# Exchanged halves of the partitions for the odd pairs of heads from the second batch on instead of from the third

## The chip, the cores and the metric

The kernel runs on one core of a Trainium2 chip. The metric is device time in microseconds (us) from the start to the end of one execution. Beside it stands the span of a profiled execution, which is the time from its first to its last instruction.

## The reference: what is computed

Four batches of eight heads go through a retention layer (attention scores with a decay and no softmax), then through two feed-forward blocks. Only the retention is touched by the change. Cut to what matters:

```python
scores = scale * np.matmul(q, k.transpose(0, 1, 3, 2))       # q, k, v: 4 x 8 x 576 x 64
gamma = 1.0 - 2.0 ** (-5.0 - np.arange(H, dtype=np.float32))
rel = pos[:, None] - pos[None, :]
Dmat = np.where(rel >= 0, gamma[:, None, None] ** rel[None, :, :], 0.0)
attn = np.matmul(scores * Dmat, v)
x = attn.transpose(0, 2, 1, 3).reshape(B * S, H * D)         # 2304 x 512
h = (x @ w1) * (x @ w2) @ w3 @ w_out
g = h @ w_in                                                 # then a leaky unit and a last product
```

## The kernel before

**How the work is tiled.** Two heads form a pair, one on partitions 0 to 63 and one on 64 to 127, so a batch has four pairs. The 576 positions of a batch are cut into five chunks, four of 128 and one of 64. The class `Retention` has three kinds of work for a chunk `c`. `scores` (L287, L276) multiplies keys by queries; VectorE then multiplies the result by the decay `mask` and gives `rt` (L291; for the last chunk `mtail` and `rte`, L279). `moments` (L302) and the state `S` (L310, L312, with the factor `gc`) carry what earlier chunks add. `values` adds two products in PSUM: state times queries (L333, 64 x 64 blocks of the array) and values times `rt` (L342). VectorE reads the PSUM tile `o` into `xs` (L349), and ScalarE and VectorE split `xs` into `xh` and `xl` for the next product.

**Where a head stands.** `places` says for each head of a pair from which partitions its operands come and to which it writes. Uncrossed, a head on partitions 0 to 63 writes to 0 to 63, and so does each pair; L333 then uses two of the four 64 x 64 blocks of the array. Crossed, the odd pairs have their heads on the other half, so that an odd and an even pair use all four. A crossed batch needs the keys, queries and last values of the odd pairs loaded in halves of 64 partitions (`in_places`, L382), and the odd pairs' columns of `mask`, `mtail` and `gc` exchanged once. That is `cross`, twelve small DMAs. Before the change batches 0 and 1 are uncrossed, and 2 and 3 crossed.

**The order of the work.** Batch 0 runs alone. Then `ab_unit` (L179) multiplies `x` by the columns of `w12`; each of its two products per column is followed by a step of the next batch's retention (`cycle`). Batch 1 has seven steps in six such places, so that its last two, for chunks 3 and 4, follow each other directly. PE, ACT and SP run in the order written; VectorE's order is made when the kernel is built. A weight of `w12` is prepared by ACT (L93, L94, L112) and VectorE (L103 to L108, L116); L112 writes its upper and L116 its lower part.

**The loads.** All go out on SP's queue. For batch 1, pairs 2 and 3 are loaded early into the room of weights (`load_apart`, tiles `pair`), pairs 0 and 1 when batch 0 has freed theirs (`load_pair`, tiles `qk` and `kv`). ACT scales the keys of a batch by `kd` (`prep`, L265). `raw` are weights as they come from HBM.

**PSUM.** Uncrossed, a chunk's `o` is one bank, and there are two of them. Crossed, it is two banks, and there is one such tile.

Of the kernel before, what the change touches and what calls it, by code (L numbers as in the profile page):

```python
# [13 lines left out]
PSUM = bass.MemoryType.PSUM  # L14
# [3 lines left out]
B, H, S, D = 4, 8, 576, 64  # L18
NPAIR = H // 2
NT, DM, DF1, DF2 = B * S, 512, 1024, 2048  # L20
CH = 128
# [116 lines left out]
def retention_moe_kernel(ctx: ExitStack, tc, qk, kv, w_out1, w3t, w12, w_in, w_out2, alpha, c_row, c_pair, out):  # L138
    nc = tc.nc

    def pool(stack, name, bufs=1, **kw):
        return stack.enter_context(tc.tile_pool(name=name, bufs=bufs, **kw))
# [20 lines left out]
    def flush():  # L163

        todo = later[:]
        later.clear()
        for step in todo:
            step()
# [17 lines left out]
    def in_wa(i, name):  # L186
        return wa.tile([P, 2, DM], F32R, tag=f"wa{i}", name=name)
# [39 lines left out]
    mtail = per_pair[:, :, 2 * CH:2 * CH + 64]  # L227
    qs = per_pair[:, :, 2 * CH + 64:]
    per_row = decay.tile([P, 128], F32, name="per_row")[:, 0:H + NPAIR]
    kd, gc = per_row[:, 0:H], per_row[:, H:]  # L230
# [11 lines left out]


    def crossed(b):
        return b >= 2

    def places(b, p):

        x = p % 2 if crossed(b) else 0
        return [(HEADS[(j + x) % 2], HEADS[j], (j + x) % 2) for j in range(2)]  # L250

    class Retention:
# [64 lines left out]
        def values(self, c):  # L317
            b, n = self.b, self.n
            w = CH if c < NCH - 1 else 64
            i0 = c * CH  # L320
            q, v, rt = qt[b], kvt[b], self.rt.pop(c)
            two = crossed(b)
            if two:
                o = self.psum["o"].tile([P, 2, 2, 2 * CH], F32, tag="o", name=f"o{b}_{c}")
                o = o[:, :, 0].rearrange("p r (i w) -> p r i w", w=CH)
            else:
                o = self.psum["o"].tile([P, NPAIR, CH], F32, tag="o", name=f"o{b}_{c}", bufs=2)
                o = o.rearrange("p (i r) w -> p r i w", r=2)
            clears = range(2 if two else 1)
            if c:  # L330
                for m, p in enumerate(self.pairs):
                    for rows, pp, _ in places(b, p):
                        nc.tensor.matmul(o[pp, p % 2, m // 2, 0:w], self.state[c - 1][rows, m],  # L333
                                         q[p][rows, i0:i0 + w],
                                         start=(m in clears), stop=False, skip_group_check=True)
            for m, p in enumerate(self.pairs):
                for j, (rows, pp, r) in enumerate(places(b, p)):
                    if c < NCH - 1:
                        vj, rj = v[p][:, 8 + 4 * j + c], rt[:, r, m]
                    else:  # L340
                        vj, rj = vt[b][p][rows], rt[rows, m]
                    nc.tensor.matmul(o[pp, p % 2, m // 2, 0:w], vj, rj, start=(c == 0 and m in clears), stop=True,  # L342
                                     skip_group_check=True)
            later.append(lambda: self.decayed(c, o, w))
# [32 lines left out]
    qt, kt, kvt, vt = ({b: {} for b in range(B)} for _ in range(4))  # L377

    def in_places(b, p, t, src):

        for rows, pp, _ in places(b, p):
            nc.sync.dma_start(out=t[rows], in_=src[pp])  # L382

    def cross():

        for p in range(1, NPAIR, 2):
            in_places(2, p, gc[:, p:p + 1], c_row[:, H + p:H + p + 1])
            for h in range(2):
                nc.sync.dma_start(out=mask[:, h, p], in_=c_pair[:, p, (1 - h) * CH:(2 - h) * CH])
            in_places(2, p, mtail[:, p], c_pair[:, p, 2 * CH:2 * CH + 64])  # L390

    def load_pair(b, p):
        x = attn.tile([P, 2, S], F32, tag=f"qk{p}", name=f"qk{b}_{p}")
        y = attn.tile([P, 17, D], F32, tag=f"kv{p}", name=f"kv{b}_{p}")
        qt[b][p], kt[b][p], kvt[b][p], vt[b][p] = x[:, 0], x[:, 1], y[:, 0:16], y[:, 16]
        if crossed(b) and p % 2:
            in_places(b, p, x, qk[b, p])
            nc.sync.dma_start(out=y[:, 0:16], in_=kv[b, p, :, 0:16])
            in_places(b, p, y[:, 16], kv[b, p, :, 16])
        else:  # L400
            nc.sync.dma_start(out=x, in_=qk[b, p])
            nc.sync.dma_start(out=y, in_=kv[b, p])
        if b == 0:
            nc.sync.dma_start(out=per_pair[:, p], in_=c_pair[:, p])

    def load_apart(b, p, n):

        x, y, z = (in_wa(n + m, f"pair{b}_{p}_{m}").bitcast(F32).rearrange("p a b -> p (a b)") for m in range(3))
        qt[b][p], kt[b][p] = x[:, 0:S], y[:, 0:S]
        vt[b][p] = x[:, S:S + D]  # L410
        kvt[b][p] = z.rearrange("p (a d) -> p a d", d=D)
        nc.sync.dma_start(out=qt[b][p], in_=qk[b, p, :, 0])
        nc.sync.dma_start(out=kt[b][p], in_=qk[b, p, :, 1])
        nc.sync.dma_start(out=kvt[b][p], in_=kv[b, p, :, 0:16])
        nc.sync.dma_start(out=vt[b][p], in_=kv[b, p, :, 16])

    def load_batch(b):
        for p in range(NPAIR):
            load_pair(b, p)

    def attention_psum(stack, twice):
        return {"sc": pool(stack, f"ps_sc{twice}", bufs=twice, space=PSUM, reuse_waits="tile"),
                "st": pool(stack, f"ps_st{twice}", space=PSUM, reuse_waits="tile"),
                "o": pool(stack, f"ps_o{twice}", space=PSUM, reuse_waits="tile") if twice == 2 else None}
# [10 lines left out]
    load_pair(0, 3)  # L435
    nc.sync.dma_start(out=al, in_=alpha)
    load_apart(1, 2, 10)
    load_apart(1, 3, 13)
    warm = psum0["o"].tile([P, 512], F32, tag="o", name="warm", bufs=2)
    for _ in range(16):  # L440
# [18 lines left out]
        flush()  # L459
    flush()  # L460
    flush()
    first.close()


    pm = pool(ctx, "pm", bufs=3, space=PSUM, reuse_waits="tile")
    pap = ExitStack()
    psum1 = attention_psum(pap, 1)
# [49 lines left out]
    def retention(b):  # L517
        r = Retention(b, list(range(NPAIR)), psum1)
        return Steps([r.prep] + r.steps())

    first_o = ExitStack()
    psum1["o"] = pool(first_o, "ps_o1", space=PSUM, reuse_waits="tile")
    r = retention(1)
    between = cycle(r, 7 / 6, 1, 6)
    for c in range(3):
# [2 lines left out]
    r.rest()  # L528
    flush()
    flush()  # L530
    first_o.close()
    psum1["o"] = pool(pap, "ps_o3", space=PSUM, reuse_waits="tile")
    cross()
    load_batch(2)
    between = cycle(None, 0, 0.6)
    for c in range(3):
# [592 lines left out]
```

## Time and profile before

| | before |
|---|---|
| three runs | 803.22, 806.06, 806.58 us; median 806.06 |
| the profiled execution | 803.67 us, span 801.9 us |
| PE busy | 787.3 us (98%) |
| PE weight loads busy | 694.1 us (87%) |
| VectorE busy | 497.7 us (62%) |
| ACT busy | 348.6 us (43%) |
| mean granted clock of PE | 0.996 |

The profiled execution lies 1.8 us outside its span and 2.4 us under the median of the runs. PE's share is an average; what a stage is worth has to be read from the waits of that stage.

### The profile page before, as it was taken

To read this page: it belongs to the slowest core of one execution; us is meant where nothing else is said; L and a number is where in the kernel's file an instruction comes from. 1 tells how busy PE (TensorE), PEld (TensorE's weight loads), DVE (VectorE), ACT (ScalarE), POOL (GpSimd) and SP (SyncE) were. 2 spreads that over 40 slices of the span, in tenths; PEclk is the share of its full clock that TensorE was granted. 3 is DMA by queue.
4 is the path that set the end of the run, shared out by engine and by line. 5 is a ranking of instruction groups with operands and counts; after the bars stand their busy time and mean duration, and the time that the engine had idled before them with its cause. 6 is when DMAs were issued, how large, how long until landed. Compare 5 with 4: busy or idle time off the path is not lost.

```text
span 801.9 us, 12688 instructions
## 1 busy us (share of the span) xinstructions
PE 787.3 (98%) x4768; PEld 694.1 (87%) x4768; DVE 497.7 (62%) x895; ACT 348.6 (43%) x648; POOL 0.2 (0%) x4
## 2 busy tenths in 40 slices
PE   7999999999999999999999999999999999999998
PEld 4778888888888988999999999999987888888886
DVE  4796785325477788988843677587899933222232
ACT  3553562231255565656514465465666622222121
POOL 0000000000000000000000000000000000000000
PEclk8999999999999999999999999999999999999999
DMA  9844931571366659899916925225557635344341
GB/s 345 344 158 125 356 135 54 165 249 54 123 193 183 198 197 336 296 388 407 387 63 221 352 101 196 108 96 202 182 196 239 218 99 177 106 132 138 99 136 41
DMA packets 81341, 156.24 MB, mean 195 GB/s; under 512 B 9600, under 2 KB 57728, under 8 KB 81280
## 3 DMA queue, kind: packets, MB, share of 16 engines
q1 hardware_dynamic: 81280, 155.43, 55.7%
q8 instruction: 37, 0.61, 0.3%
q14 instruction: 24, 0.20, 0.1%
HBM read 104.02 MB, written 51.38 MB: 194 GB/s over the span
## 4 chain that ended last, share of the span: by engine, by line
PE 89%; DVE 5%; DMA 2%; ACT 1%; issue 1%; SPq 1%; ACTq 0%; DVEq 0%
PE ps L179 25%; PE o L1044 23%; PE h L883 18%; PE y L816 12%; PE pw L630 5%; PE o L342 2%; PE sc L287 2%; DMA raw<-in_w_dram 1%; PE o L333 1%; PE st L302 1%; DMA gr<-gd 0%; DVE gl L173 0%; DVE xs L349 0%; DMA xs<-x2d 0%; DVE rt L291 0%
## 5 line engine op out<-in xcount | busy, mean ns | idle before, releaser
L179 PE MATMUL ps<-xh,w 128*128 128x512 f32 (+1 forms) x640 | 186.0, 372 | 2.0 <-ACT w L112 1.6
L1044 PE MATMUL o<-wb,gh 128*128 128x512 f32 x576 | 177.6, 389 | 0.9 <-ACT gh L172 0.9
L179 PEld LDWEIGHTS ps<-xh,w 128*128 128x128 f32 x640 | 116.0, 189 | 23.6 <-ACT w L112 1.8
L1044 PEld LDWEIGHTS o<-wb,gh 128*128 128x128 f32 x576 | 108.1, 188 | 23.8 <-ACT gh L172 1.4
L179 PE MATMUL ps<-xl,w 128*128 128x512 f32 (+1 forms) x320 | 118.0, 369 | 0.0
L1044 PE MATMUL o<-wb,gl 128*128 128x512 f32 x288 | 112.3, 390 | 0.4 <-DVE gl L173 0.4
L173 DVE TENSOR_TENSOR gl<-gr,gh 128x768 fp32r<-128x768 f32 x48 | 46.0, 958 | 99.9 <-ACT gh L172 99.8
L816 PE MATMUL y<-yab,wp 128*128 128x384 f32 x576 | 100.0, 334 | 0.0
L816 PEld LDWEIGHTS y<-yab,wp 128*128 128x128 f32 x576 | 99.9, 188 | 0.1
L172 ACT CAST gh<-gr 128x768 fp32r<-128x768 f32 x48 | 40.2, 838 | 115.9 <-PE o L1044 112.6
L179 PEld LDWEIGHTS ps<-xl,w 128*128 128x128 f32 x320 | 60.4, 189 | 9.8 <-DVE xl L173 0.3
L1044 PEld LDWEIGHTS o<-wb,gl 128*128 128x128 f32 x288 | 54.1, 188 | 12.3 <-DVE gl L173 1.3
L895 DVE SCALAR_TENSOR_TENSOR g<-m,al,g 128x384 f32<-128x384 f32 x48 | 29.7, 618 | 48.9 <-ACT g L894 45.8
L883 PE MATMUL h<-xT,wv 128*128 128x384 f32 x288 | 54.9, 334 | 1.5 <-DVE g L901 1.5
L883 PE MATMUL h<-xT,wu 128*128 128x384 f32 x288 | 55.0, 335 | 0.5 <-ACT h L908 0.3
L883 PEld LDWEIGHTS h<-xT,wv 128*128 128x128 f32 x288 | 50.3, 188 | 1.8 <-DVE g L901 1.8
L108 DVE CUSTOM_DVE_ANT_0 a<-a,b 128x1024 uint16<-128x1024 uint16 x72 | 49.5, 688 | 3.5
L883 PEld LDWEIGHTS h<-xT,wu 128*128 128x128 f32 x288 | 50.2, 188 | 1.1 <-ACT h L908 0.6
L487 ACT CAST ab<-f 128x512 fp32r<-128x512 f32 (+1 forms) x40 | 23.1, 577 | 63.1 <-DVE f L491 54.5
L103 DVE TENSOR_SCALAR a<-a 128x512 f32<-128x512 f32 x72 | 30.4, 422 | 25.7 <-ACT a L93 25.4
L491 DVE TENSOR_TENSOR f<-f,ps 128x512 f32<-128x512 f32 (+1 forms) x40 | 25.3, 632 | 31.6 <-PE ps L179 31.3
L630 PE MATMUL pw<-wo,w 128*128 128x512 f32 x192 | 44.1, 390 | 0.0
(95 smaller groups left out, 1007.5 us busy)
## 6 DMA issues: line engine op xcount, KB each, us to landing
gd<-g SPq DMA_DIRECT2D x96, 192.0 KB, 1.9
gr<-gd SPq DMA_DIRECT2D x96, 192.0 KB, 2.6
abd<-ab SPq DMA_DIRECT2D x32, 512.0 KB, 4.3
raw<-in_w_out_dram SPq DMA_DIRECT2D x24, 512.0 KB, 3.7
yab<-abd SPq DMA_DIRECT2D x24, 384.0 KB, 7.9
raw<-in_w_dram SPq DMA_DIRECT2D x16, 512.0 KB, 7.1
raw<-in_w3t_dram SPq DMA_DIRECT2D x16, 512.0 KB, 4.1
rawi<-in_w_in_dram SPq DMA_DIRECT2D x16, 512.0 KB, 6.3
```

The costliest lines, as they stand in the source:

```text
L103: nc.vector.tensor_scalar(out=a, in0=a, scalar1=self.LEAST, scalar2=self.MOST, op0=ALU.max, op1=ALU.min)
L108: nc.vector.tensor_tensor(out=a.bitcast(I32), in0=a.bitcast(I32), in1=b, op=ALU.add)
L172: nc.scalar.copy(hi, src)
L173: nc.vector.tensor_tensor(out=lo, in0=src, in1=_f32(hi), op=ALU.subtract)
L179: nc.tensor.matmul(ps, a, bb, start=(n == 0), stop=(n == last))
L487: nc.scalar.copy(t[:, 0], f)
L491: nc.vector.tensor_tensor(out=f, in0=f, in1=pss[1], op=ALU.mult)
L630: nc.tensor.matmul(acc[i], a[:, ic], bb, start=(k == 0 and n == 0), stop=(k == C1 - 1 and n == 2))
L816: nc.tensor.matmul(ys[o], wpc[c][a][:, oc], yab[b, c][:, bb], start=(c == 0 and i == 0), stop=(c == C1 - 1 and i == 2))
L883: nc.tensor.matmul(ps, a[:, x, ks], b[:, y, k], start=(fresh and n == 0), stop=(n == 5), skip_group_check=True)
L895: nc.vector.scalar_tensor_tensor(out=g, in0=r, scalar=neg[:, c:c + 1], in1=g, op0=ALU.mult, op1=ALU.add)
L1044: nc.tensor.matmul(accs[b][i], x[:, m, ic], y, start=(j == 0 and m == 0 and q == 0), stop=(j == C1 - 1 and m == 1 and q == 2))
```

## The change

`crossed` is true from batch 1 on. `cross` is called when batch 0 is done, ahead of the first `ab_unit`, and no longer after batch 1. `load_apart` loads queries, keys and last values in halves, those of the even pair 2 too. The one PSUM pool for `o` with two banks serves batches 1 to 3.

```diff
     def crossed(b):
-        return b >= 2
+        return b >= 1
...
     def cross():

         for p in range(1, NPAIR, 2):
-            in_places(2, p, gc[:, p:p + 1], c_row[:, H + p:H + p + 1])
+            in_places(1, p, gc[:, p:p + 1], c_row[:, H + p:H + p + 1])
             for h in range(2):
                 nc.sync.dma_start(out=mask[:, h, p], in_=c_pair[:, p, (1 - h) * CH:(2 - h) * CH])
-            in_places(2, p, mtail[:, p], c_pair[:, p, 2 * CH:2 * CH + 64])
+            in_places(1, p, mtail[:, p], c_pair[:, p, 2 * CH:2 * CH + 64])
...
-        nc.sync.dma_start(out=qt[b][p], in_=qk[b, p, :, 0])
-        nc.sync.dma_start(out=kt[b][p], in_=qk[b, p, :, 1])
+        in_places(b, p, qt[b][p], qk[b, p, :, 0])
+        in_places(b, p, kt[b][p], qk[b, p, :, 1])
         nc.sync.dma_start(out=kvt[b][p], in_=kv[b, p, :, 0:16])
-        nc.sync.dma_start(out=vt[b][p], in_=kv[b, p, :, 16])
+        in_places(b, p, vt[b][p], kv[b, p, :, 16])
...
     flush()
     flush()
+    cross()
     first.close()
...
-    first_o = ExitStack()
-    psum1["o"] = pool(first_o, "ps_o1", space=PSUM, reuse_waits="tile")
+    psum1["o"] = pool(pap, "ps_o3", space=PSUM, reuse_waits="tile")
     r = retention(1)
...
-    first_o.close()
-    psum1["o"] = pool(pap, "ps_o3", space=PSUM, reuse_waits="tile")
-    cross()
     load_batch(2)
```

PE and ACT keep their order. On SP's queue, the loads of batch 1's pair 2 stood so before (`pair_2_0` holds queries and last values, `pair_2_1` keys, `pair_2_2` the rest; what a row waits for stands in brackets, and `DMAHW0` to `DMAHW7` count the landings of every eighth DMA):

```order
L412 DMA pair_2_0_134<-in_qk_dram 128x576 [waits DMAHW0_49]
L413 DMA pair_2_1_135<-in_qk_dram 128x576 [waits DMAHW1_49]
L414 DMA pair_2_2_136<-in_kv_dram 128x1024 [waits DMAHW2_49]
L415 DMA pair_2_0_134<-in_kv_dram 128x64 [waits DMAHW3_49]
L412 DMA pair_3_0_141<-in_qk_dram 128x576 [waits DMAHW4_49]
```

The same place of SP's queue now, for pair 2:

```order
L382 DMA pair_2_0_134<-in_qk_dram 64x576 [waits DMAHW0_49]
L382 DMA pair_2_0_134<-in_qk_dram 64x576 [waits DMAHW1_49]
L382 DMA pair_2_1_135<-in_qk_dram 64x576 [waits DMAHW2_49]
L382 DMA pair_2_1_135<-in_qk_dram 64x576 [waits DMAHW3_49]
L414 DMA pair_2_2_136<-in_kv_dram 128x1024 [waits DMAHW4_49]
L382 DMA pair_2_0_134<-in_kv_dram 64x64 [waits DMAHW5_49]
L382 DMA pair_2_0_134<-in_kv_dram 64x64 [waits DMAHW6_49]
```

Three loads of 128 partitions became six of 64; each waits for the DMA eight places ahead of it. Pair 3 is changed in the same way, and pair 1's load of `qk` is cut in two and that of `kv` in three.

SP's queue behind the load of batch 1's pair 1, now (the load of the large part of `kv_1` stands eight DMAs ahead of the second `64x64` row below, and its landing is what `DMAHW6` counts there; `per_row` is the tile of `gc`, and `per_pair` that of `mask` and `mtail`):

```order
L382 DMA per_row<-const_row_dram 64x1 [waits DMAHW1_49,DVE_49]
L382 DMA per_row<-const_row_dram 64x1 [waits DMAHW2_49]
L389 DMA per_pair<-const_pair_dram 128x128 [waits DMAHW3_49,DVE_49]
L389 DMA per_pair<-const_pair_dram 128x128 [waits DMAHW4_49]
L382 DMA per_pair<-const_pair_dram 64x64 [waits DMAHW5_49,DVE_49]
L382 DMA per_pair<-const_pair_dram 64x64 [waits DMAHW6_49]
L382 DMA per_row<-const_row_dram 64x1 [waits DMAHW7_49,DVE_49]
L382 DMA per_row<-const_row_dram 64x1 [waits DMAHW0_49]
L389 DMA per_pair<-const_pair_dram 128x128 [waits DMAHW1_49,DVE_49]
L389 DMA per_pair<-const_pair_dram 128x128 [waits DMAHW2_49]
```

These rows stood ahead of batch 2's loads before; they now stand between batch 1's loads and the seventh piece of `raw`. The waits on `DVE` are for batch 0's last reads of the tables.

VectorE's queue where batch 1's first scores are masked (`rt_0`), before:

```order
L491 TENSOR_TENSOR f_0_488<-f_0_488,ps_0_1_522 128x512 [waits PE_49,Activation_49]
L291 TENSOR_TENSOR rt_0_538<-sc_0_537,per_pair 128x1024 [waits PE_49]
L103 TENSOR_SCALAR a_518<-a_518 128x512 [waits Activation_49]
L308 COPY S_0_611<-st_0_547 128x256 [waits PE_49]
L483 TENSOR_TENSOR ab_0_489<-f_0_488,ab_0_489 128x512 [waits Activation_49]
L116 TENSOR_TENSOR w_2_558<-a_484,w_2_558 128x512 [waits Activation_49]
```

The same rows of VectorE's queue now:

```order
L492 TENSOR_TENSOR f_0_509<-f_0_509,ps_0_1_543 128x512 [waits PE_49,Activation_49]
L291 TENSOR_TENSOR rt_0_559<-sc_0_558,per_pair 128x1024 [waits DMAHW3_49,DMAHW2_49,DMAHW4_49,DMAHW1_49,PE_49]
L103 TENSOR_SCALAR a_539<-a_539 128x512 [waits Activation_49]
L308 COPY S_0_632<-st_0_568 128x256 [waits PE_49]
L484 TENSOR_TENSOR ab_0_510<-f_0_509,ab_0_510 128x512 [waits Activation_49]
L116 TENSOR_TENSOR w_2_579<-a_505,w_2_579 128x512 [waits Activation_49]
```

The order is the same, and `rt_0` waits for four more landings: the exchanged columns of `mask`.

## Rows read from the trace of the kernel before

**Rows 1.** Windows: us, busy us (instructions) of each engine, granted clock, DMA share, GB/s
```profile
38.90:62.00 23.10, 21.25 (x247) 17.25 (x246) 22.62 (x41) 11.67 (x22) 0.00 (x0) 1.00 0.41 138
69.00:190.00 121.00, 121.00 (x818) 99.14 (x817) 66.52 (x113) 46.75 (x87) 0.00 (x0) 1.00 0.52 179
```

**Rows 2.** Timeline of PE: start, us, instruction, count, idle time before it and releaser
```profile
42.09 0.50 PE L179 MATMUL ps<-xh,w 128*128 128x512 f32 x1 [1.61 <-ACT w L112]
...
43.06 0.50 PE L179 MATMUL ps<-xh,w 128*128 128x512 f32 x1 [0.23 <-DVE w L116]
```

**Rows 3.** Timeline of ACT, 36 to 42 us
```profile
36.58 1.71 ACT L265 ACTIVATE kv<-kv,per_row 128x256 f32<-128x256 f32 x4
...
41.42 0.62 ACT L112 CAST w<-a 128x512 fp32r<-128x512 f32 x1
```

**Rows 4.** Timeline of VectorE at batch 1's first masked scores
```profile
39.91 1.23 DVE L291 TENSOR_TENSOR rt<-sc,per_pair 128x1024 f32<-128x1024 f32 x1 [0.34 <-PE sc L287]
```

**Rows 5.** Timeline of PE, batch 1, chunk 1: state times queries, then values
```profile
52.19 0.65 PE L333 MATMUL o<-qk,S 64*64 64x128 f32 x8
...
53.21 0.66 PE L342 MATMUL o<-rt,kv 128*64 128x128 f32 x8
```

**Rows 6.** Timeline of PE, batch 2 (crossed), the same chunk
```profile
126.09 0.67 PE L333 MATMUL o<-qk,S 64*64 64x128 f32 x16
126.69 1.09 PE L342 MATMUL o<-rt,kv 128*64 128x128 f32 x16
```

**Rows 7.** Timeline of VectorE at the end of batch 1's chunk 3
```profile
66.90 0.69 DVE L349 TENSOR_TENSOR xs<-o,per_pair 128x512 f32<-128x512 f32 x1 [0.46 <-PE o L342]
```

**Rows 8.** Timeline of PE, the first product after batch 1
```profile
68.08 0.50 PE L179 MATMUL ps<-xh,w 128*128 128x512 f32 x1 [0.15 <-ACT xh L172]
```

**Rows 9.** Timeline of SP's queue, three of its first DMAs
```profile
5.11 0.49 SPq L85 DMA_DIRECT2D raw<-in_w_dram  x1
...
13.55 0.33 SPq L412 DMA_DIRECT2D pair<-in_qk_dram  x1
...
26.82 0.38 SPq L402 DMA_DIRECT2D kv<-in_kv_dram  x1
```

**Rows 10.** DMA issues at 5.11 and 26.82: KB, us from issue to landing
```profile
raw<-in_w_dram SPq DMA_DIRECT2D x1, 512.0 KB, 8.4
...
kv<-in_kv_dram SPq DMA_DIRECT2D x1, 544.0 KB, 10.2
```

**Rows 11.** Windows: batch 1's loads, and half loads of batch 2
```profile
30.00:36.00 6.00, 5.37 (x60) 4.19 (x56) 4.54 (x14) 2.24 (x5) 0.00 (x0) 1.00 1.02 415
78.70:81.40 2.70, 2.70 (x14) 2.23 (x13) 2.58 (x5) 0.62 (x1) 0.00 (x0) 1.00 0.99 256
```

**Rows 12.** DMA issues, batch 2's pair 1: its two halves of keys and queries
```profile
qk<-in_qk_dram SPq DMA_DIRECT2D x1, 288.0 KB, 6.1
...
qk<-in_qk_dram SPq DMA_DIRECT2D x1, 288.0 KB, 6.8
```

**Rows 13.** Timeline of SP's queue: the exchange of tables, and those halves
```profile
69.69 0.59 SPq L382 DMA_DIRECT2D per_pair<-const_pair_dram  x1
...
71.61 1.06 SPq L389 DMA_DIRECT2D per_pair<-const_pair_dram  x2
...
74.98 1.12 SPq L382 DMA_DIRECT2D qk<-in_qk_dram  x2
```

**Rows 14.** DMA issues at 72.2: the second pair's columns of the mask
```profile
per_pair<-const_pair_dram SPq DMA_DIRECT2D x2, 64.0 KB, 2.1
```

**Rows 15.** Window at the start
```profile
10.60:17.30 6.70, 5.93 (x48) 4.72 (x48) 5.61 (x13) 3.06 (x6) 0.00 (x0) 0.50 1.03 419
```

**Rows 16.** Timeline of PE at the start
```profile
10.40 0.68 PE L287 MATMUL sc<-qk 64*128 64x128 f32 x4 [2.10 <-DMA qk<-in_qk_dram]
...
13.06 1.23 PE L287 MATMUL sc<-qk 64*128 64x128 f32 x8
...
18.50 0.71 PE L287 MATMUL sc<-qk 64*128 64x128 f32 x8
```

## The prediction

> **What bounds the kernel now.** I read the windows first, then the waits of TensorE (PE) where the change acts, and then what those waits hang on. From 69 to 190 us PE is busy 121.00 of 121.00 us [rows 1]: behind batch 1 nothing can absorb a delay, and what is gained or lost by 69 us stays to the end. Batch 1's retention runs from 38.7 to 67.8 us. There VectorE is as full as PE: 22.62 of 23.10 us between 38.9 and 62 [rows 1], so it cannot catch up either. PE's two waits of that stretch stand in its timeline: 1.61 us for ACT's upper part of a weight, up to 42.09, and 0.23 us for VectorE's lower part, up to 43.06 [rows 2]. VectorE's lower part comes a few instructions behind batch 1's first masked scores (`rt_0`), which start at 39.91 when PE's scores are done [rows 4]. The order of VectorE shows `rt_0` ahead of that weight both before and now, so whatever holds `rt_0` holds the weight and PE. The third thing to see is the queue of loads. The DMA engines are full while batch 1's data come in: 415 GB/s from 30 to 36 us, at a share of 1.02 [rows 11].
>
> **What the change gains.** State times queries of a chunk took 53.21 - 52.19 = 1.02 us uncrossed [rows 5], and 126.69 - 126.09 = 0.60 us crossed [rows 6]: 0.42 us less. Chunks 1, 2 and 3 have it in full, 1.26 us. Scores, moments and the product of values keep their shapes, and I cost them at nothing. Chunk 4 follows chunk 3 directly, and there is now one `o` tile where there were two. So PE can start chunk 4 only when VectorE has read chunk 3, which ended at 66.90 + 0.69 = 67.59 [rows 7]. Before, PE's next product started 0.49 us after that read, at 68.08, held by ACT's `xh` [rows 8]; chunk 4 was done in the meantime. Now chunk 4 lies between. At half the columns I take it as half of a chunk's 0.60 us and of the product of values behind it, about 0.7 us, and 0.1 us for the signal: 0.8 us against 0.49, a loss of 0.3 us. The gain is 1.26 - 0.3, about 0.95 us. The twelve table DMAs leave SP's queue at 67 us and batch 2's loads start about 7 us earlier. That is worth nothing, since PE has no idle time there to win back.
>
> **What the change costs: the mask comes late.** `rt_0` now waits for the exchanged columns of `mask`, and these stand in SP's queue behind batch 1's loads, which get longer.
>
> First, how that queue runs. A DMA waits for the landing of the one eight places ahead: the ninth, issued at 5.11, took 8.4 us to land, 13.5, and the seventeenth was issued at 13.55 [rows 9, 10]. The last large load of batch 1, `kv_1`, was issued at 26.82 and landed 10.2 us later, at 37.0 [rows 9, 10]. As the engines are full all that time, every added us of transfer moves that landing.
>
> Second, what is added. Pair 1's `qk` becomes two halves of 288 KB on 64 partitions, and four loads of pairs 2 and 3 become eight of 144 KB. At 415 GB/s a half of 288 KB takes 0.71 us. Batch 2 shows such halves: issued about 0.5 us apart from 74.98 on [rows 13], they took 6.1 and 6.8 us to land [rows 12], so the second landed 1.2 us after the first. Throughput in their stretch is 256 GB/s with the engines still full, a share of 0.99 [rows 11]. So a half costs about 0.5 us more than its bytes, two of them 1.0 us; the smaller ones I take at half of that, 8 x 0.25 = 2.0 us. The last values go out as 16 KB pieces; no row prices them apart, and I take 0.4 us, from 0 to 0.8. Together 3.4 us. The lower bound is 0, if halves that follow each other share the engines fully; the upper is that a half takes as long as the whole it came from, 2 x 0.71 + 8 x 0.355 + 0.8 = 5.1 us. I take 3.4, nearest to the measured halves.
>
> The Trainium skill, SBUF — State Buffer, section "Door 1: The DMA port swizzle (why `[64,N]` ≈ `[32,N]`)", says that 64 partitions reach only 8 of 16 ports, about 218 of 436 GB/s, and its section on issuing two DMAs for both halves reports only 6% gained from a pair. The 256 GB/s of the trace agrees in direction and is somewhat higher; by the page's rate alone the 3.4 us would be 5.1, and the predicted time 812.7.
>
> Third, from there to the mask. `kv_1` lands at 37.0 + 3.4 = 40.4. The second 64 x 64 piece of pair 1's `mtail` waits for exactly that landing, and gc and mask of pair 3 are behind it. Before, that same piece was issued at 69.69, the second half of pair 3's mask at about 72.2 [rows 13], and it took 2.1 us to land [rows 14]: 72.2 + 2.1 - 69.7 = 4.6 us. So the mask is there at 45.0, and `rt_0` starts 5.1 us later than 39.91 (from 1.7 us with nothing added, to 6.8 us at the upper bound). Queued behind it on VectorE are the weight's lower part, the state of chunk 0, and the next weights; PE's third matmul of the next product moves from 43.06 to about 48.2. ACT is late too but hidden: its scaling of keys waits for `kv_1` at 40.4; from 36.58 to the upper part of the weight at 41.42 are 4.8 us [rows 3], less 0.85 us for pair 0, whose keys come earlier, so that is ready at 44.4. From 48.2 on PE and VectorE run as they did from 43.1.
>
> **The clock.** PE stands for most of 9.5 us, from 38.7 to 48.2, with about 2.2 us of scores, moments and two matmuls in between. At the start, a wait of 2.10 us up to 10.40 [rows 16] was followed by a granted clock of 0.50 from 10.6 to 17.3 us [rows 15], the lower of two levels, and eight scores took 1.23 us there against 0.71 later [rows 16]. The 1.61 us wait at 40.5 was not followed by a fall: 1.00 up to 62 [rows 1]. I expect a fall here. A stretch like that of the start, 6.7 us, would cost at most half of it, 3.4 us, if it lay wholly on PE's work; part of it will lie in the wait. I take 2.0 us, between 0 and 3.4.
>
> **The sum.** -0.95 + 5.1 + 2.0 = +6.15 us on the profiled execution's 803.67 us: 809.8. The median of the runs, 806.06, is 2.4 us above that execution; the three runs lie on both sides of it, so I add half of this and predict 811.0 us.
>
> **The rivals**, each on the same footing (803.67 + 1.2 us):
> - *Late mask, full clock.* If the pieces of work in the long wait hold the clock, the 2.0 us fall away: +4.15 us, 809.0. For it: 1.00 after the 1.61 us wait. Against it: the fall at the start came after a wait barely longer.
> - *Halves at the upper bound and a longer low clock.* `rt_0` 6.8 us late and 3.0 us for the clock: +8.85, 813.7. For it: 256 GB/s is already an average with the end of a whole load in it. Against it: the second half landed 1.2 us after the first, not 1.42. The rule of the Trainium skill, SBUF — State Buffer, section "Door 1: The DMA port swizzle (why `[64,N]` ≈ `[32,N]`)", is this case for the halves.
> - *Not slower: the halves overlap.* Eight DMAs are in flight, so engines that are done with one half may take the next, on the other 64 partitions, and nothing is added. `kv_1` lands at 37.0, the mask at 41.6, `rt_0` is 1.7 us late, the clock holds: 1.7 - 0.95 = +0.75 us, 805.6, within the bound below. With a full clock it decides from the point where the mask lands before 39.91 + 0.95 + 4.0 = 44.9. Against it: batch 2's halves had the same neighbours and did not overlap.
> - *Faster.* The mask lands before 39.9: -0.95 us, 803.9. SP's wait for `kv_1` plus the 4.6 us behind it speak against that even at full rate.
>
> **How the numbers follow.** Half a per cent, 4.0 us, is about what a measurement of this kernel tells from no change. The forecast has 0.50, the full clock 0.15, the upper bound 0.17, the overlap 0.15, faster 0.03. Forecast and upper bound are slower, of the full clock one half: 0.50 + 0.17 + 0.07 = 0.74. Within the bound: the overlap and the other half, 0.23. The range of 805.0 to 816.0 reaches from just under the overlap to above the upper bound with a low clock of 3.4 us and the median's full 2.4 us (6.8 - 0.95 + 3.4 + 806.06 = 815.3).
>
> **What would show it.** In the profile after: state times queries at about 0.60 us per chunk in batch 1; half loads of batch 1 with the engines full at well under 415 GB/s; `kv_1` landing past 40 us; `rt_0` waiting for a DMA of `per_pair`, to about 45 us; PE waiting some 5 us more for that weight; a granted clock of 0.50 somewhere between 42 and 55 us; a wait on VectorE's `xs` ahead of chunk 4; and no new PE wait from there to 190 us. The prediction is wrong if `kv_1` lands by 38 us, if `rt_0` doesn't wait, or if the loss is made up behind 69 us.

## The result, and the profile after

The changed kernel takes 813.25 us (median of 6 runs, 812.34 to 813.87), the kernel before beside it 805.79 us (803.22 to 809.48): a ratio of 1.0088, 95% interval 1.0067 to 1.0108. It is slower. The profiled execution took 813.87 us with a span of 812.1 us, 10.2 us over that of before. PE was busy 789.5 us where it was 787.3 us, so most of the difference is waiting and not work.

The windows of the changed kernel (columns as in [rows 1]) show where:

```profile
20.00:30.00 10.00, 8.53 (x144) 6.82 (x142) 8.05 (x24) 3.56 (x9) 0.00 (x0) 1.00 0.87 260
...
38.70:44.00 5.30, 1.98 (x19) 1.43 (x20) 0.69 (x1) 0.92 (x3) 0.00 (x0) 0.97 0.59 144
44.00:48.00 4.00, 2.79 (x16) 1.87 (x16) 0.00 (x0) 4.00 (x10) 0.00 (x0) 0.50 0.17 32
48.00:52.00 4.00, 1.22 (x2) 0.50 (x2) 3.00 (x5) 1.73 (x4) 0.00 (x0) 0.50 0.48 153
52.00:56.00 4.00, 3.85 (x9) 3.08 (x10) 3.86 (x10) 1.33 (x3) 0.00 (x0) 0.50 0.29 73
56.00:62.00 6.00, 6.00 (x60) 4.73 (x60) 4.79 (x10) 2.54 (x5) 0.00 (x0) 0.89 0.31 128
...
78.00:200.00 122.00, 122.00 (x850) 99.98 (x841) 67.64 (x114) 47.43 (x89) 0.00 (x0) 1.00 0.54 179
```

Three things are to be seen. From 20 to 30 us batch 1's loads run at 260 GB/s with the DMA engines at 0.87 of their time. The same window of the kernel before reads:

```profile
20.00:30.00 10.00, 9.28 (x160) 7.55 (x156) 8.21 (x25) 3.90 (x10) 0.00 (x0) 1.00 1.04 414
```

So 1.54 MB less came in during those 10 us, which at 414 GB/s is 3.7 us of loading. Then PE works 2.0 of the 5.3 us from 38.7, and its granted clock is 0.50 from 44 to 56. Behind the retention nothing is made up: 122.00 of 122.00 us busy, as in [rows 1].

SP's timeline of the changed kernel, with the issue of `kv_1` and of the last columns of `mask`:

```profile
31.58 0.53 SPq L398 DMA_DIRECT2D kv<-in_kv_dram  x1
...
46.19 1.00 SPq L389 DMA_DIRECT2D per_pair<-const_pair_dram  x2
```

Its row among the DMA issues, which answers to [rows 10] (KB, us from issue to landing):

```profile
kv<-in_kv_dram SPq DMA_DIRECT2D x1, 512.0 KB, 12.3
```

`kv_1` is issued 4.76 us later than the 26.82 of [rows 9], and then takes 12.3 us to land against 10.2 in [rows 10]; that is 43.9, 6.9 us later than before. What waits for it is in ACT's timeline, which answers to [rows 3]:

```profile
43.98 0.91 ACT L265 ACTIVATE kv<-kv,per_row 128x256 f32<-128x256 f32 x2 [2.73 <-DMA kv<-in_kv_dram]
...
48.00 0.61 ACT L112 CAST w<-a 128x512 fp32r<-128x512 f32 x1
```

VectorE's timeline, which answers to [rows 4] and [rows 7]:

```profile
49.00 1.23 DVE L291 TENSOR_TENSOR rt<-sc,per_pair 128x1024 f32<-128x1024 f32 x1 [9.49 <-DMA per_pair<-const_pair_dram]
...
77.00 0.69 DVE L349 TENSOR_TENSOR xs<-o,per_pair 128x512 f32<-128x512 f32 x1
```

`rt_0` waits 9.49 us and starts 9.1 us later than 39.91. PE's timeline, which answers to [rows 2], [rows 5] and [rows 8]:

```profile
41.84 0.49 PE L287 MATMUL sc<-qk 64*128 64x128 f32 x2 [2.71 <-DMA qk<-in_qk_dram]
...
48.66 0.80 PE L179 MATMUL ps<-xh,w 128*128 128x512 f32 x1 [1.65 <-ACT w L112]
...
52.15 1.22 PE L179 MATMUL ps<-xh,w 128*128 128x512 f32 x2 [2.26 <-DVE w L116]
...
58.09 0.66 PE L342 MATMUL o<-rt,kv 128*64 128x128 f32 x8
...
63.66 0.45 PE L333 MATMUL o<-qk,S 64*64 64x128 f32 x8
...
64.26 0.66 PE L342 MATMUL o<-rt,kv 128*64 128x128 f32 x8
...
77.75 0.34 PE L333 MATMUL o<-qk,S 64*64 64x64 f32 x8 [0.79 <-DVE xs L349]
...
78.37 0.50 PE L179 MATMUL ps<-xh,w 128*128 128x512 f32 x1
```

The third matmul of the next product stands at 52.15, 9.09 us late; chunk 0's product of values at 58.09 where before it stood at 46.64, 11.45 us late. From chunk 1 on the lateness shrinks: 64.26 against the 53.21 of [rows 5] is 11.05, and chunks 2 and 3 come 10.58 and 10.10 us late (70.38 and 75.86 against 59.80 and 65.76). At the end PE waits 0.79 us for `xs`, and the first product behind the retention is 10.29 us late against [rows 8]. From there to the end of the span both kernels take the same, 733.7 us now and 733.8 before.

### The profile page after: what moved, and what is told of

It is laid out like the page before. It is cut to its first block, busy times and chain, and to the rows that moved or that the text cites. A ratio compares the mean times of both kernels' runs of the same rounds, so it can differ in the third digit from the quotient of the medians.

```text
span 812.1 us, 12703 instructions
## 1 busy us (share of the span) xinstructions
PE 789.5 (97%) x4768; PEld 695.3 (86%) x4768; DVE 498.7 (61%) x895; ACT 349.6 (43%) x648; POOL 0.2 (0%) x4
## 4 chain that ended last, share of the span: by engine, by line
PE 87%; DMA 5%; DVE 4%; ACT 1%; SPq 1%; issue 1%; ACTq 0%; DVEq 0%
PE ps L179 24%; PE o L1041 23%; PE h L880 18%; PE y L813 12%; PE pw L627 5%; PE o L342 2%; DMA kv<-in_kv_dram 2%; PE sc L287 2%; DMA gr<-gd 1%; DMA raw<-in_w_dram 1%; PE o L333 1%; PE st L302 1%; DMA xs<-x2d 1%; DVE rt L291 0%; DVE g L898 0%
## 5 line engine op out<-in xcount | busy, mean ns | idle before, releaser
L179 PE MATMUL ps<-xh,w 128*128 128x512 f32 (+1 forms) x640 | 187.9, 375 | 3.9 <-DVE w L116 2.3
```

The lines of the kernel that those rows point to most:

```text
L179: nc.tensor.matmul(ps, a, bb, start=(n == 0), stop=(n == last))
```

## The experiments

Three theories stood at the start. **A**: the half loads of batch 1 hold up the queue; everything else follows from late data. **B**: what costs is the place of `cross`, so that the mask is late by itself. **C**: the crossed layout costs, by its single `o` tile or in PE. Unless an edit says otherwise, PE, ACT and VectorE keep the order of the kernel that the edit starts from.

### Halves only

The kernel before; batch 1 is loaded in halves as after the change, and nothing is crossed.

```diff
-        if crossed(b) and p % 2:
+        if (crossed(b) or b == 1) and p % 2:
...
-        nc.sync.dma_start(out=qt[b][p], in_=qk[b, p, :, 0])
-        nc.sync.dma_start(out=kt[b][p], in_=qk[b, p, :, 1])
+        in_places(b, p, qt[b][p], qk[b, p, :, 0])
+        in_places(b, p, kt[b][p], qk[b, p, :, 1])
...
-        nc.sync.dma_start(out=vt[b][p], in_=kv[b, p, :, 16])
+        in_places(b, p, vt[b][p], kv[b, p, :, 16])
```

> The kernel before, with batch 1's loads cut into halves of 64 partitions as in the changed kernel, and nothing crossed. Theory A (the half loads are the loss): the large load of pair 1 lands near 43.9 us as in the changed kernel (37.0 before), ACT's scaling waits for it, and the weight's upper part comes at 48.0 instead of 41.4, its lower part near 49.3. PE's third matmul of the next product moves from 43.1 to about 49.4 us, +6.3, and with a granted clock of 0.50 behind that wait some 2.4 more: +8.7 us, about 812.4. Rival B (the late mask is the loss, the half loads are hidden by themselves): at most +1 us.

Measured: 813.11 us, ratio 1.0098 (1.0073 to 1.0123). A holds. Its windows and, below them, ACT's timeline:

```profile
20.00:30.00 10.00, 8.90 (x152) 7.17 (x148) 8.20 (x24) 3.81 (x10) 0.00 (x0) 1.00 0.85 250
...
48.00:52.00 4.00, 2.34 (x8) 1.66 (x7) 3.09 (x8) 3.30 (x7) 0.00 (x0) 0.50 0.00 0
```

```profile
45.52 0.91 ACT L265 ACTIVATE kv<-kv,per_row 128x256 f32<-128x256 f32 x2 [2.51 <-DMA kv<-in_kv_dram]
```

Throughput is that of the changed kernel, and `kv_1` comes 8.5 us late. No mask is exchanged here: `rt_0` waits for PE's scores and starts at 46.04. In the times the late data alone give the whole loss. In this execution the first product behind the retention starts at 77.63, 9.55 us late; the other 2.1 us of its longer span lie behind that point.

### Tables early

The kernel before; the twelve DMAs of `cross` are issued once more at the new place, with the values that the tables already have.

```diff
-    def cross():
+    def cross(b=2):
...
+                g = 1 - h if crossed(b) else h
-                nc.sync.dma_start(out=mask[:, h, p], in_=c_pair[:, p, (1 - h) * CH:(2 - h) * CH])
+                nc.sync.dma_start(out=mask[:, h, p], in_=c_pair[:, p, g * CH:(g + 1) * CH])
...
+    cross(1)
     first.close()
```

> The kernel before, with the twelve small table loads also issued behind batch 1's loads, with the values the tables have already; loads whole, nothing crossed. Theory A: the large load of pair 1 lands at 37.0 as before, the mask 4.9 us later at 41.9, the first masked scores start 2.0 us later than 39.9: +2.0 us, and +2.4 more if the granted clock falls. Rival B (the place of the tables is the loss): the masked scores wait as long as in the changed kernel, some +9 us.

Measured: 805.67 us, ratio 1.0012 (0.9993 to 1.0031). VectorE's timeline of this run:

```profile
40.93 1.23 DVE L291 TENSOR_TENSOR rt<-sc,per_pair 128x1024 f32<-128x1024 f32 x1 [1.35 <-DMA per_pair<-const_pair_dram]
```

The mask is late by itself, by 1.0 us where 2.0 were expected. So with whole loads B is about a tenth of the loss, and in the times it cannot be told.

### Whole loads

The changed kernel, but the odd pairs of batch 1 stand exchanged in the layout of the input already, so that its loads are whole again.

```diff
-        if crossed(b) and p % 2:
+        if b >= 2 and p % 2:
...
-        in_places(b, p, qt[b][p], qk[b, p, :, 0])
+        nc.sync.dma_start(out=qt[b][p], in_=qk[b, p, :, 0])
...
+    def exchanged(a):
+        a = by_pair(a).copy()
+        a[1, 1::2] = a[1, 1::2, ::-1]
+        return a
```

> The changed kernel, with batch 1's loads whole again: keys, queries and last values of its odd pairs lie exchanged in HBM already, so everything is crossed and the tables are still exchanged at the new place. Theory A: pair 1's load lands at 37.0, the mask at 41.9, the masked scores 2.0 us late; the crossing gains 1.2: +0.8 us on the kernel before (804.5), or +3.2 if the granted clock falls. Rival B: the mask stays late by itself and most of the changed kernel's +7 to +10 us remains. Rival C (the crossed layout itself, with one o tile, costs): more than +3 us at a full clock.

Measured: 804.88 us, ratio 0.9995 (0.9977 to 1.0013). PE's timeline:

```profile
43.33 0.73 PE L179 MATMUL ps<-xh,w 128*128 128x512 f32 x2 [0.55 <-DVE w L116]
...
52.45 0.45 PE L333 MATMUL o<-qk,S 64*64 64x128 f32 x8
...
53.05 0.66 PE L342 MATMUL o<-rt,kv 128*64 128x128 f32 x8
```

Everything of the change but the halves is in this run, and the loss is gone: C falls. State times queries takes 0.60 us, and the crossed chunk 1 stands at 53.05 against 53.21 before although the third matmul of the next product came 0.27 us later. The first product behind the retention starts at 67.39, 0.69 us ahead of before: with the granted clock at 1.00 the crossing gains 0.96 us.

### Which loads

Three runs start from the changed kernel and make part of batch 1's loads whole. In the first the even pair 2 is loaded whole; it needed no halves.

```diff
-        in_places(b, p, qt[b][p], qk[b, p, :, 0])
+        whole = lambda b, p, t, src: nc.sync.dma_start(out=t, in_=src)
+        load = in_places if p % 2 else whole
+        load(b, p, qt[b][p], qk[b, p, :, 0])
...
```

> The changed kernel, with pair 2 (even, not exchanged) loaded whole; pairs 1 and 3 stay in halves. Theory A: four of the eight small halves and two small pieces less, about a quarter to a third of the delay of 6.9 us: pair 1's large load lands near 42.2 instead of 43.9, the masked scores start near 47.2 instead of 49.0, -1.8 us on the changed kernel. Rival (only the last halves count, those of pair 1, since the earlier ones have time to spare): no change, under 0.5 us.

Measured: 811.48 us, ratio 1.0085 (1.0058 to 1.0112); `kv_1` reaches ACT at 41.35, and chunk 0's product of values stands at 55.21, 2.9 us earlier than in the changed kernel. In the times no gain can be told, as the changed kernel's ratio is 1.0088.

In the second, pairs 2 and 3 are whole (pair 3 by the layout) and only pair 1 comes in halves; in the third it is the other way round.

```diff
-        in_places(b, p, qt[b][p], qk[b, p, :, 0])
+        nc.sync.dma_start(out=qt[b][p], in_=qk[b, p, :, 0])
...
+        a[1, 3] = a[1, 3, ::-1]
```

> The changed kernel, with the loads of pairs 2 and 3 whole; only pair 1's keys, queries and last values still come in halves. The half loads delay the landing of kv_1 in sum by 6.9 us in the changed kernel's trace (43.9 against 37.0). If the halves of pairs 2 and 3 are most of it, as pair 2 alone gave back 2.6 us, kv_1 lands at about 43.9 - 2 x 2.6 = 38.7, rt_0 starts at about 43.6, and chunk 0's product of values at 50 to 52 us (46.64 before, 58.09 changed): 808 us, ratio 1.002 to 1.006. If pair 1's halves, the last ones ahead of kv_1, are most of it, kv_1 lands past 41 and the ratio stays at 1.007 or more.

```diff
-        if crossed(b) and p % 2:
+        if b >= 2 and p % 2:
...
+        a[1, 1] = a[1, 1, ::-1]
```

> The counterpart: pair 1 whole, pairs 2 and 3 in halves. If the halves of pairs 2 and 3 are most of the loss, SP's issue of kv_1 and its landing come at most 2 us earlier than in the changed kernel, kv_1 lands at 42 to 43, and the ratio is 1.006 to 1.009. If pair 1's halves are most of it, kv_1 lands before 40 and the ratio is below 1.004.

Measured: pair 1 alone 809.98 us, ratio 1.0061 (1.0039 to 1.0083); pairs 2 and 3 alone 811.97 us, ratio 1.0087 (1.0053 to 1.0121). ACT's timeline with pair 1 alone in halves, and its VectorE:

```profile
39.63 0.91 ACT L265 ACTIVATE kv<-kv,per_row 128x256 f32<-128x256 f32 x2 [2.40 <-DMA kv<-in_kv_dram]
```

```profile
44.77 1.23 DVE L291 TENSOR_TENSOR rt<-sc,per_pair 128x1024 f32<-128x1024 f32 x1 [5.45 <-DMA per_pair<-const_pair_dram]
```

ACT's timeline with pairs 2 and 3 alone in halves:

```profile
43.41 0.91 ACT L265 ACTIVATE kv<-kv,per_row 128x256 f32<-128x256 f32 x2 [1.93 <-DMA kv<-in_kv_dram]
```

The small halves of pairs 2 and 3 delay `kv_1` by 6.4 us, pair 1's large ones by 2.6 us. The shares are rough: they add up to 9.0 us where the changed kernel has 6.9, and nearly the same queue of loads brought `kv_1` to ACT between 43.98 and 46.13 us in four executions. The two kinds of halves also slow the loads in different ways. A window with pair 1 alone in halves, while they come in behind the end of a whole load:

```profile
32.00:36.00 4.00, 3.61 (x24) 2.99 (x23) 2.82 (x9) 2.00 (x5) 0.00 (x0) 1.00 1.04 239
```

A window with pairs 2 and 3 alone in halves:

```profile
20.00:30.00 10.00, 9.70 (x162) 7.80 (x160) 8.04 (x24) 3.56 (x10) 0.00 (x0) 1.00 0.77 208
```

With pair 1's halves the DMA engines stay full at a lower rate; with the small ones they also stand idle, at a share of 0.77. The run with pair 1 alone took 2 us more than expected: its clock fell too (0.50 from 44 to 52 us), so the loss does not shrink in step with the lateness.

### Small loads on all partitions

The kernel before, with as many loads as in the run of the halves and the same bytes in each, but keys and queries cut by columns, so that each piece covers 128 partitions. The 16 KB pieces stay halves.

```diff
+            if b == 1:
+                nc.sync.dma_start(out=x[:, 0], in_=qk[b, p, :, 0])
+                nc.sync.dma_start(out=x[:, 1], in_=qk[b, p, :, 1])
...
+        for m in range(4):
+            x, s = (qt, kt)[m // 2][b][p], slice(m % 2 * (S // 2), (m % 2 + 1) * (S // 2))
+            nc.sync.dma_start(out=x[:, s], in_=qk[b, p, :, m // 2, s])
```

> The kernel before, with the same number of loads and the same bytes in each as in the run that only cut batch 1's loads in halves, but keys and queries cut by columns: each piece still covers all 128 partitions. If it is the 64 partitions that cost, the DMA engines keep above 390 GB/s from 20 to 30 us, kv_1 lands by 38 us and the time stays within 0.3% of before. If it is the number of loads, with eight in flight, throughput from 20 to 26 us falls to about 250 GB/s as with halves, kv_1 lands past 43 and the ratio is about 1.01.

Measured: 807.67 us, ratio 1.0038 (1.0023 to 1.0053), between the two. Windows and ACT's timeline:

```profile
20.00:30.00 10.00, 8.78 (x152) 7.05 (x150) 8.22 (x25) 3.43 (x9) 0.00 (x0) 1.00 0.95 311
```

```profile
39.01 0.91 ACT L265 ACTIVATE kv<-kv,per_row 128x256 f32<-128x256 f32 x2 [1.89 <-DMA kv<-in_kv_dram]
```

With 128 partitions the same number of loads runs at 311 GB/s, against 250 with 64 and 414 whole, and `kv_1` is about 2.0 us late instead of 8.5. Neither theory of its expectation holds by itself: most of the delay is gone when the pieces cover 128 partitions, and 2.0 us of it stay. Why is not shown, as more than the partitions differs. Pieces cut by columns have rows half as long in HBM, so the 2.0 us may hold a part that the halves don't pay. SP also issues them faster, pair 3's four pieces in 2.56 us from 20.30 us on, where the run of halves only took 2.98 us. So the gain may come from the transfer or from the issue.

### Masks first

The changed kernel; in `cross` the four DMAs of `mask` go ahead of those of `gc` and `mtail`.

```diff
+            for h in range(2):
+                nc.sync.dma_start(out=mask[:, h, p], in_=c_pair[:, p, (1 - h) * CH:(2 - h) * CH])
+        for p in range(1, NPAIR, 2):
             in_places(1, p, gc[:, p:p + 1], c_row[:, H + p:H + p + 1])
-            for h in range(2):
...
```

> The changed kernel, with the four loads of the exchanged mask columns ahead of those of gc and mtail. Theory A (SP's queue, where each load waits for the one eight places ahead, adds 4.9 us between pair 1's landing and the mask): the last mask load is issued when pair 1's first half has landed, near 41.8, and lands at about 44.6 instead of 48.8. Then ACT's upper part of the weight, at 48.6, is what ends last, and PE's third matmul moves from 52.1 to about 49.4: -2.8 us on the changed kernel. Rival (the transfers themselves set the mask's landing, not SP's queue): no change.

Measured: 812.51 us, ratio 1.0107 (1.0083 to 1.0132), no gain that can be told. VectorE, ACT and PE:

```profile
47.28 1.23 DVE L291 TENSOR_TENSOR rt<-sc,per_pair 128x1024 f32<-128x1024 f32 x1 [7.29 <-PE st L302]
```

```profile
46.13 0.91 ACT L265 ACTIVATE kv<-kv,per_row 128x256 f32<-128x256 f32 x2 [1.67 <-DMA kv<-in_kv_dram]
```

```profile
50.83 0.80 PE L179 MATMUL ps<-xh,w 128*128 128x512 f32 x1 [1.66 <-ACT w L112]
...
51.85 1.05 PE L179 MATMUL ps<-xh,w 128*128 128x512 f32 x2
```

The last columns of `mask` land at 47.16, 1.1 us behind `kv_1` instead of 4.9. So most of the 4.9 us was SP's queue, as theory A says, and the rival falls. Those columns are still what `rt_0` waits for: the profile puts its wait to PE's `st`, which it doesn't read, while the scores were done at 46.49. But PE's third matmul no longer waits for VectorE, and the wait for ACT's upper part takes its place, as expected.

The gain that doesn't show in the times is in the trace. In this execution `kv_1` came 2.2 us later than in the changed kernel. From the start of its scaling on ACT to PE's third matmul it took 51.85 - 46.13 = 5.72 us, with halves only 51.22 - 45.52 = 5.70, and in the changed kernel 52.15 - 43.98 = 8.17. So behind late loads the tables at their new place cost some 2.5 us, and not only the 1.0 us that they cost with whole loads.

### Whole loads and masks first

Both edits together.

> Both edits: whole loads from a layout that is exchanged in HBM, and the mask's loads first. Theory A: pair 1 lands at 37.0, the mask near 37.7, ahead of 39.9, so that nothing waits that did not wait before; what is left is the crossing's own gain: -1.2 us on the kernel before, 802.5 beside 803.7, with the granted clock at 1.00. Rival C (the crossed layout with one o tile costs): the same as before or slower.

Measured: 803.41 us, ratio 0.9991 (0.9979 to 1.0004): the best median of all, and not to be told from before. A window and PE:

```profile
44.00:48.00 4.00, 4.00 (x22) 2.88 (x22) 3.86 (x8) 2.33 (x5) 0.00 (x0) 0.57 0.53 158
```

```profile
42.20 0.50 PE L179 MATMUL ps<-xh,w 128*128 128x512 f32 x1 [1.64 <-ACT w L112]
...
48.28 0.66 PE L342 MATMUL o<-rt,kv 128*64 128x128 f32 x8
```

`rt_0` no longer waits (it starts at 40.00). Yet chunk 0 stands 1.64 us later than before, because the granted clock fell to 0.57 behind the 1.64 us wait for ACT. The gain of crossing won 1.2 us of that back: the first product behind the retention starts at 68.51, 0.43 us later than before.

### PE kept busy

The changed kernel, with 24 matmuls in PE's waits whose results nobody reads: 10 between the first scores of pairs 0 and 1, 6 ahead of the next product and 8 behind its second matmul. VectorE's order changed here too: the weight's lower part comes ahead of `rt_0`.

```diff
+                if b == 1 and c == 0 and m == 1:
+                    keep_busy(10)
...
+                if n == 2 and stop_at:
+                    keep_busy(stop_at)
...
+            if (n, c, m) == (0, 1, 0):
+                keep_busy(6)
```

> The changed kernel, with 24 matmuls whose result nobody reads put into PE's three long waits (10 between pair 0's and pair 1's first scores, 6 ahead of the next product, 8 behind its second matmul). They add 5.4 us of PE work that fits into the waits. Theory (the fall of the granted clock is a cost of its own, 2.4 us): the clock stays at 1.00 through 44 to 58 us, PE's third matmul stays near 52.1, and the masked product of chunk 0 comes 2.4 us earlier, near 55.7 instead of 58.1: -2.4 us on the changed kernel. Rival (at a full clock PE would only wait for VectorE instead): no gain, under 0.5 us.

Measured: 812.23 us, ratio 1.0094 (1.0071 to 1.0118); in medians not to be told from the changed kernel. Its trace is clear, though (L188 is the product, L355 the product of values):

```profile
51.75 0.61 PE L188 MATMUL ps<-xh,w 128*128 128x512 f32 x2
...
55.20 0.66 PE L355 MATMUL o<-rt,kv 128*64 128x128 f32 x8
```

The clock is 1.00 in every window from 38.7 to 62 us. From the third matmul of the product to chunk 0's product of values it takes 3.45 us, against 58.09 - 52.15 = 5.94 in the changed kernel: the low clock costs 2.5 us there, in agreement with 11.45 - 9.09 = 2.4 above. With the 0.4 us that the third matmul comes earlier (51.75 against 52.15) that is the whole of the shorter span, 809.2 us against 812.1. The clock was perhaps not held in every execution: two of the four runs took 811.01 and 809.31 us at a mean granted clock of 0.995, the other two 814.04 and 813.44 us at 0.991.

## Why the prediction was right, and what it mis-sized

**The sign and the place hold; that the size does is partly luck.** 811.0 us was predicted, with a range of 805.0 to 816.0 that contains 813.25. But the main term of the sum came out at twice its size. In profiled executions +6.15 us was predicted and +10.2 measured. The medians differ by 7.5 us only, because that of before lies 2.1 us above its profiled execution and that of the changed kernel 0.6 us below.

**The gain of crossing: 0.95 us predicted, 1.2 measured** (0.96 with whole loads). State times queries went from 1.02 to 0.60 us per chunk. The lateness fell by 0.40, 0.47 and 0.48 us over chunks 1 to 3, 1.35 in sum; the wait for `xs` ahead of chunk 4 took 0.19 us back where 0.3 was expected.

**The half loads: 3.4 us predicted, 6.9 measured.** This is the term that was mis-sized, above the prediction's upper bound of 5.1. `kv_1` landed at 43.9, not 40.4. The step that failed is "as the engines are full all that time, every added us of transfer moves that landing": the share was 0.87 from 20 to 30 us, so the queue lost time in which nothing was transferred, beside halves that ran slower. The runs show which loads did it. The small halves of pairs 2 and 3, put at 2.0 us, cost 6.4 alone, and there the engines were not full; pair 1's, put at 1.0, cost 2.6 with the engines full from 32 to 36 us, so there mainly the price was wrong; the last values, put at 0.4 for all pairs, are in both.

Why the engines idle is not isolated, but SP's queue narrows it down. Each DMA waits for the one eight ahead of it, and so eight pieces of 16 and 144 KB hold fewer bytes in flight than eight whole loads. Up to 20 us that held SP in both kernels. Before, the last load of pair 3 went out at 20.47 us; now only the first halves of pair 3 go out then (SP's timeline of before, and below it that of the changed kernel):

```profile
20.47 0.44 SPq L415 DMA_DIRECT2D pair<-in_kv_dram  x1
```

```profile
20.64 3.47 SPq L382 DMA_DIRECT2D pair<-in_qk_dram  x4
```

From there to the issue of `kv_1` no landing holds SP. The waits of its queue from 20.7 to 32 us in the changed kernel are all for compute engines (us in total, times, longest):

```profile
SPq L402 <- PE st L302: 0.6, 1, 0.6
SPq L85 <- ACT xh L172: 0.5, 1, 0.5
SPq L398 <- PE o L342: 0.3, 1, 0.3
```

SP issues one DMA behind the other there, four halves of 144 KB in 3.47 us, and the engines fall to a share of 0.65 from 22 to 24 us. So in that stretch the engines idle while SP is issuing, not while it waits for the landing eight places ahead. That its time for each half starves them is read from this order; no run changed it alone. Batch 2's pair 1, from which the price was taken, had two halves between whole loads and so did not show it.

The Trainium skill, SBUF — State Buffer, section "Door 1: The DMA port swizzle (why `[64,N]` ≈ `[32,N]`)", gives 64 partitions half of the 16 ports. The run cut by columns agrees that the partitions matter: 250 GB/s with 64, 311 with 128. It doesn't show that ports are why. At the 218 GB/s that the prediction takes from the Trainium skill, its halves come to an estimated 4.65 us with 0.8 for the last values; its 5.1 takes half of the measured 415 GB/s.

**From `kv_1` to the mask: 4.6 us predicted, 4.9 measured** (the last columns were issued at about 46.7 and took 2.1 us, 48.8). So `rt_0` came 9.1 us late and not 5.1, and PE's third matmul with it. ACT's upper part was started at 48.00, 3.6 us behind the 44.4 of the prediction (which calls that time ready, though 41.42 in [rows 3] is a start too), by the same lateness of `kv_1`; it was hidden behind `rt_0` as expected. With halves and no mask exchanged it was the last (50.21 us for PE's first matmul), and so it was with masks first: of the 9.1 us only some 2.5 go before ACT's wait takes over.

**The clock: 2.0 us predicted, 2.4 measured,** with a granted clock of 0.50 between 44 and 56 us.

**The sum.** In profiled executions: -1.2 + 9.1 + 2.4 = +10.3 us against a span 10.2 us longer; predicted was +6.15. In medians the loss is 7.5 us. The prediction's 1.2 us for the median of before came out as 2.1 (805.79 - 803.67), while the profiled execution of after is the slowest of its six runs. The runs of the kernel before differ with their clock: of 55 runs beside the experiments, 22 had a mean granted clock of 0.995 or more and took 802.69 to 805.09 us, and 33 had 0.994 or less and took 804.49 to 807.65. The profiled execution of before, at 0.996, is one of the first kind. Where the clock fell in the others is open, as no trace of them is kept. Traces of the other runs show two candidates. One is the wait for ACT that before also has: the fall behind it cost 1.6 us in the run with both edits. The other lies near 625 us, far from the change: windows of before and of masks first.

```profile
620.00:640.00 20.00, 20.00 (x90) 16.57 (x89) 19.32 (x34) 12.76 (x21) 0.00 (x0) 1.00 0.73 242
```

```profile
620.00:640.00 20.00, 17.57 (x70) 13.76 (x69) 16.23 (x29) 11.27 (x19) 0.00 (x0) 0.91 0.72 254
```

Masks first took 737.0 us from its first product behind the retention to the end, and halves only, which shows the same fall, 735.9, against 733.8 before. The changed kernel, with a granted clock of 1.00 there, took 733.7.

**The rivals.** The overlap of halves falls with the run of halves only, and the full clock with the 0.50 from 44 to 56 us. The upper bound came nearest to the size, and its own term was still too small. That scores could be masked without an exchanged `mask` was not tried.

## What to carry to other kernels

A change of layout that is free for the engines is paid where the data are loaded: count the DMAs it adds to the queue ahead of the first reader, and see whether the loads are in a stretch with slack (batches 2 and 3 here) or one that bounds the start of a stage (batch 1). Price a run of small partition halves from a run of them, not from a pair between whole loads, and prefer to change the layout of the input, which here took the loss away entirely, though no gain in time could be told either. When DMA engines idle, read what the queue that issues waits for. When two late things stand one behind the other, removing the one that the trace names shows the next; and an execution whose data land later can hide what the edit gained.

## What the runs showed of the hardware

- Nearly the same queue of loads brought `kv_1` to ACT at 43.98, 44.65, 45.52 and 46.13 us in four executions (the change, PE kept busy, halves only, masks first); in before and in the runs with whole loads the landing left no wait to see.
- The granted clock stayed at 1.00 behind a 1.61 us wait of PE in the kernel before and with whole loads and behind one of 1.63 us with tables early, and fell to 0.57 (44 to 48 us) behind one of 1.64 us with whole loads and masks first, and to 0.61 behind one of 1.81 us with loads cut by columns. Waits that differ by hundredths of a us went either way.
